# First phase of an attention kernel: x loaded ahead of the values' weights, their scales taken later

## The chip, the cores and the metric

The kernel runs on one core of a Trainium2 chip. The metric is the device time of one execution in microseconds (us), the median of repeated runs. The core's engines are named as the profile names them: PE (TensorE, matrix products), DVE (VectorE), ACT (ScalarE), POOL (GpSimd) and SP (SyncE, which here only issues DMAs).

## The reference, cut to what matters

```
x: (1, 2048, 640), wqkv: (640, 1920), wo: (640, 640), two sets A and B, gate_w: (640)
g = sigmoid((x * gate_w).sum(-1, keepdims=True))
attention(x, wqkv, wo):            # 32 heads of 20 columns
    q, k, v = split of x @ wqkv
    p = softmax(q @ k.T * 20 ** -0.5)
    return (p @ v, heads side by side) @ wo
out = g * attention(x, wqkv_A, wo_A) + (1 - g) * attention(x, wqkv_B, wo_B)
```

Everything is float32, and both attentions read the same x.

## The kernel before

**Numbers.** Matrix products of float32 data are made from float16 pairs. A tensor is multiplied by a power of two that its largest absolute value sets, and split into a high and a low half; a product takes three float16 products (high by high, low by high, high by low). The scale needs a maximum over the whole tensor, so it can't be known before all of the tensor has arrived. The generator `scales` turns a column of per-partition maxima into scales: PE transposes the column (L173), DVE reduces it and forms the power of two and its inverse in six small instructions (L177 to L183), PE spreads both over all partitions (L190), DVE copies them out (L193). It yields `PRODUCT` ahead of each of its two PE steps, so that a caller can place other work between.

**Order.** The program is written out by hand, engine by engine: each engine's instructions run in the order in which the code issues them, and waits follow from the data. There are seven PSUM banks (`take`, `give`): a small model of the engines' clocks chooses which bank is used next; it does not change the order.

**First phase.** SP issues the loads: the first columns of the queries' and keys' weights (`ws`), the values' weights of the first eight heads (`wv`, 160 columns, the 161st is `gate_w`), then x in eight pieces (`xs`). DVE takes maxima as the pieces land (`largest`, L234). One call of `scales` then serves five columns: queries, keys, values, gate and x. From then on PE transposes x (L869, 80 blocks; 24 of them ahead of the scales), ACT writes the scaled high half `xh` (L873) and DVE the low half `xl` (L874).

**Products of the first phase.** `a_chunk(ch)` makes keys and part of the queries of the first four heads for 512 of the 2048 rows: 15 products in one bank, then ACT writes the high half into the staging tile `cq` (L417), DVE the low half (L418), and DMAs spread `cq` into `KT` and `QT` (`kt`, `qt` in the profile), alternately from SP (L428, both halves) and POOL (L430, the high half). Two chunks share one `cq` tile, of which there are two. `r_chunk(ch, ...)` makes the rest of the queries (`rk`) in the same way. `differences_of(half, ...)` forms, on POOL, the differences of two chunks' keys (`fd`, `dd`, L468 to L472) and spreads them into `KD` (`kd`). The order is `a_chunk` 0, 1, 2 (with x's remaining transposes between), `r_chunk(0)`, `a_chunk(3)`, the second differences, and `split_now` for `wv` on ACT and POOL.

**Maxima.** Sixteen groups of four products of queries and keys follow (`max_mm`, L581), each in turn with about six products of the remaining `r_chunk`s and of `project_v`, the values' projection. ACT writes the positive part of one product (L585), DVE adds the other and takes the maximum (L589). The values' projection needs the two halves of `wv`, `wvh` and `wvl`.

**Main loop.** After that a loop of 512 steps makes scores, exponentials and weighted values, with projections and output products filled in. It ends with the output's last rows.

**Constant rows.** Four rows of a constant (`mrow`, in a buffer of the `cq` tag) are copied by four POOL DMAs into rows 60 to 63 and 124 to 127 of both `KT` tiles.

Of the kernel before, what the change touches and what calls it, by code (L numbers as in the profile page):

```python
# [14 lines left out]
OP = mybir.AluOpType  # L15
AX = mybir.AxisListType
# [3 lines left out]
P = 128  # L20
S = 2048
D = 640
# [39 lines left out]
PRODUCT = "product"  # L62
# [6 lines left out]
def kernel(  # L69
# [10 lines left out]
    nc = tc.nc  # L80
# [22 lines left out]
    KT = [consts.tile([P, 2, S], F16, name=f"kt{i}") for i in range(2)]  # L103
# [6 lines left out]
    inv_x = consts.tile([P, 1], F32, name="inv_x")  # L110
    inv_g = consts.tile([P, 1], F32, name="inv_g")
# [17 lines left out]
    def take():  # L129

        i = min((k for k in range(NB) if k not in held), key=lambda k: free_at[k])
        held.add(i)
        return i, banks[i]

    def spend(engine, cost, ready=0.0):

        clock[engine] = max(clock[engine], ready) + cost
        return clock[engine] + T_BACK

    def give(i, t):  # L140
        free_at[i] = t
        held.discard(i)
# [7 lines left out]
    def tick_block(cost, ready=0.0):  # L150

        begin = block_end[0] if now[0] < 0 and block_end[1] == rows_free else max(rows_free) + T_MODE
        clock["pe"] = max(begin, ready)
        rows_free[:] = [clock["pe"] + cost + T_MODE] * 2
        block_end[:] = [clock["pe"] + cost, list(rows_free)]
        clock["done"] = clock["pe"] + cost + T_READY - T_MODE


    def powers(ei, n):

        c = [slice(k * n, (k + 1) * n) for k in range(5)]
        nc.vector.tensor_scalar(ei[:, c[1]], ei[:, c[0]], 0x7F800000, None, op0=OP.bitwise_and)
        nc.vector.tensor_scalar(ei[:, c[2]], ei[:, c[1]], float(20 << 23), None, op0=OP.max)
        nc.vector.tensor_scalar(ei[:, c[3]], ei[:, c[2]], -1.0, float((254 + XE) << 23), op0=OP.mult, op1=OP.add)
        nc.vector.tensor_scalar(ei[:, c[4]], ei[:, c[2]], float(XE << 23), None, op0=OP.subtract)

    def scales(maxima, n, then):

        for _ in range(REST):
            yield  # L170
        yield PRODUCT
        i, pt = take()
        nc.tensor.transpose(pt[:n, :P], maxima[:, :n], ident)  # L173
        tick_block(0.1, free_at[i])
        yield
        e = wts.tile([5, 8], F32, name="e", tag="scl", bufs=2)
        nc.vector.tensor_reduce(e[:n, 0:1], pt[:n, :P], axis=AX.X, op=OP.max)  # L177
        give(i, spend("dve", 0.3, clock["done"]))
        spend("dve", 1.0)
        powers(e.bitcast(I32)[:n, :], 1)  # L180
        dg = wts.tile([5, 2, 5], F32, name="dg", tag="scd", bufs=2)
        for k in range(2):
            nc.vector.tensor_scalar(dg[:n, k, :n], ident[:n, :n], e[:n, 3 + k:4 + k], None, op0=OP.mult)  # L183
        for _ in range(REST):
            yield
        yield PRODUCT
        i, pb = take()
        tick_block(0.1, free_at[i])
        for k in range(2):
            nc.tensor.matmul(pb[:, k * n:(k + 1) * n], ones[:n, :], dg[:n, k, :n], start=True, stop=True)  # L190
        yield
        both = wts.tile([P, 10], F32, name="both", tag="scb", bufs=2)
        nc.vector.tensor_copy(both[:, :2 * n], pb[:, :2 * n])  # L193
        give(i, spend("dve", 0.2, clock["done"]))
        then(both[:, :n], both[:, n:2 * n])
# [12 lines left out]
    def set_v(gg, r, inv):  # L208
        nc.vector.tensor_copy(r_v[gg], r)

        f = gg % (NG // 2) * 160
        while f < (gg % (NG // 2) + 1) * 160:
            p0 = f % P
            n = min(P - p0, (gg % (NG // 2) + 1) * 160 - f, (P, 32, 64, 32)[p0 // 32])
            nc.vector.tensor_copy(wrow[gg // (NG // 2)][p0:p0 + n, f // P:f // P + 1], inv[p0:p0 + n])
            f += n
# [16 lines left out]
    def largest(dst, src):  # L233
        nc.vector.tensor_reduce(dst, src, axis=AX.XY, op=OP.max,  # L234
                                apply_absolute_value=True)
        spend("dve", 0.5)
# [82 lines left out]
    def split_now(t, r, hi, lo):  # L319
        nc.scalar.activation(hi, t, AF.Copy, scale=r)  # L320
        nc.gpsimd.tensor_scalar(t, t, r, None, op0=OP.mult)
        nc.gpsimd.tensor_tensor(lo, t, hi, op=OP.subtract)  # L322
# [97 lines left out]
    def run(gen):  # L420
        for _ in gen:
            pass
# [415 lines left out]
    wv = start.tile([P, NC, 161], F32, name="wv")  # L838
    w_t = wqkv[0].rearrange("(c p) f -> p c f", p=P)
    for part in range(2):  # L840
        nc.sync.dma_start(ws[:, part], w_t[:, :, part * D:part * D + 320])
    nc.sync.dma_start(wv[:, :, :160], w_t[:, :, 2 * D:2 * D + 160])
    for i in range(0, NT, 2):
        nc.sync.dma_start(xs[:, i:i + 2, :], x_t[:, i:i + 2, :])
    nc.scalar.dma_start(wv[:, :, 160], gate_w.rearrange("(c p) -> p c", p=P))
    mrow = wts.tile([P, S], F16, name="mrow", tag="cq", bufs=2)[:4]
    nc.gpsimd.memset(mrow, MS)
    for i in range(2):
        for j in range(2):
            nc.gpsimd.dma_start(KT[i][64 * j + 60:64 * j + 64], mrow.unsqueeze(1).to_broadcast([4, 2, S]))  # L850
    for i in range(2):
        nc.gpsimd.memset(V[i][:, :, :, DH:VW], 1.0)
    xm = start.tile([P, 8], F32, name="xm")
    wm = start.tile([P, 5], F32, name="wm")
    for part in range(2):
        largest(wm[:, part:part + 1], ws[:, part])
    largest(wm[:, 2:3], wv[:, :, :160])
    largest(wm[:, 3:4], wv[:, :, 160:161])
    for i in range(8):
        largest(xm[:, i:i + 1], xs[:, 2 * i:2 * i + 2, :])  # L860
    nc.vector.tensor_reduce(wm[:, 4:5], xm, axis=AX.X, op=OP.max)

    def turn(j0, c):

        n = slice(j0 * P, (j0 + 4) * P)
        i, pt = take()
        for u in range(4):
            tick_block(0.11, free_at[i])
            nc.tensor.transpose(pt[:, u * P:(u + 1) * P], xs[:, j0 + u, c * P:(c + 1) * P], ident)  # L869

        def drain():
            give(i, spend("dve", T_MAX, spend("act", T_EXP, clock["done"])))
            nc.scalar.activation(xh[:, c, n], pt, AF.Copy, scale=r_x)  # L873
            nc.vector.scalar_tensor_tensor(xl[:, c, n], pt, r_x, xh[:, c, n], op0=OP.mult, op1=OP.subtract)  # L874

        return drain

    def turns_of(j0, cs=range(NC)):
        for c in cs:
            turn(j0, c)()  # L880
            yield
# [3 lines left out]
    load()  # L885
    drains = [turn(0, c) for c in range(NC)] + [turn(4, 0)]
    found = []
    run(scales(wm, 5, lambda r, inv: found.extend((r, inv))))
    r, inv = found
    r_x = r[:, 4:5]  # L890
    hi, lo = blk["a", 0] = block_tiles("a")
    split_now(ws[:, 1, :, 0:GF], r[:, 1:2], hi[:, :, 0:GF], lo[:, :, 0:GF])
    split_now(ws[:, 0, :, 0:48], r[:, 0:1], hi[:, :, GF:P], lo[:, :, GF:P])
    for f in drains:
        f()
    hi, lo = blk["r", 0] = block_tiles("r")
# [3 lines left out]
    nc.gpsimd.tensor_copy(hi.rearrange("p c (j f) -> p c j f", j=4), w_r)  # L900
    nc.gpsimd.tensor_tensor(lo.rearrange("p c (j f) -> p c j f", j=4), w_r, hi.rearrange("p c (j f) -> p c j f", j=4),
                            op=OP.subtract)
    nc.vector.tensor_copy(inv_x, inv[:, 4:5])
    halves = []
    both = cycle((nc.sync, nc.gpsimd))

    def a_chunk(ch):
        if ch % 2 == 0:
            halves.append(half_tiles(0))
        n = slice((ch % 2) * QB, (ch % 2 + 1) * QB)  # L910
        hl = halves[ch // 2][:, :, n]
        yield from project_chunk(blk["a", 0], hl[:, 0], hl[:, 1], ch)
        for pair in range(2):
            run(spread(0, hl, ch * QB, QB, q=(0,) if ch == pair == 0 else (), k=(pair,), queues=both))

    def r_chunk(ch, pairs):
        yield from project_r(0, ch)
        n = slice((ch % 2) * QB, (ch % 2 + 1) * QB)
        run(spread(0, halves[ch // 2][:, :, n], ch * QB, QB, q=pairs, k=(), queues=both))
        spread_done.add((0, ch))  # L920

    def beside(gen, n, other):

        for k, _ in enumerate(gen):
            if k % n == n - 1:
                next(other, None)
        run(other)
# [10 lines left out]
    beside(a_chunk(1), 3, turns_of(8))  # L938
    differences_of(0, KD[0])
    beside(a_chunk(2), 3, turns_of(12))  # L940
    run(r_chunk(0, (1,)))
    run(a_chunk(3))
    differences_of(1, KD[1])
    hi, lo = v_tiles(0)
    split_now(wv[:, :, :160], r[:, 2:3], hi[:, :, :160], lo[:, :, :160])
    split_now(wv[:, :, 160:161], r[:, 3:4], hi[:, :, 160:161], lo[:, :, 160:161])
    nc.vector.tensor_scalar(inv_g, inv[:, 3:4], inv_x, -1.0, op0=OP.mult, op1=OP.mult)
    set_qk(0, r[:, 0:2], inv[:, 0:2])
    set_v(0, r[:, 2:3], inv[:, 2:3])
    split_next()  # L950
    rest = series(*(r_chunk(ch, (0, 1)) for ch in (1, 2, 3)), *(project_v(0, j) for j in range(0, NT, 2)))

# [13 lines left out]
    chain = finish_max(0, 0)  # L966
# [25 lines left out]
    for g in range(2 * NG):  # L992
        b = g * step
        n = g + 1
        if n < 2 * NG:
# [5 lines left out]
            i = g // 4 + 1  # L1001
            if i < 4:
                if g % 4 == 0:
                    z, c0 = i // 2, 320 * (i % 2)
                    srcs = max_tasks([[(wqkv[z], part * D + c0 + 160 * k) for k in range(2)] for part in range(2)],
                                     lambda m, i=i: scales_qk(i, m))
# [105 lines left out]
    for G in range(STEPS + 1):  # L1112
        g, qb, i = unit_of(G)
# [12 lines left out]
        for what in (STEP[blocks] if maxima or some else LATE + " X" * (blocks == 2)).split():  # L1126
            k = count[what] = count.get(what, 0) + 1
            if what[0] == "e":
                q = sum(count.get(f"e{j}", 0) for j in range(2)) - 1
                j = int(what[1])  # L1130
# [55 lines left out]
```

## Time and profile before

| | before |
|---|---|
| median of 3 runs | 2802.12 us (2801.08 to 2802.19) |
| the profiled execution's own time | 2800.33 us |
| its span | 2798.5 us, 61863 instructions |
| granted PE clock, mean | 0.995 |
| busy: PE, DVE, ACT, POOL | 98%, 88%, 90%, 24% |

The page gives the busy time of each engine and the chain of work that ended last. Since the change touches only the first phase, the views with a time window are of most use: the timeline (when each instruction began, how long it took, and in brackets how long its engine was idle ahead of it and what ended that), the chain of waits in order of time, and the table of stretches with the granted PE clock and the DMA rate.

### The profile page before, as it was taken

Reading aid. Unit: us, or ns where it says so; the run is one execution under the profiler, and the core shown is the slowest. Engines: PE = TensorE matmul, PEld = TensorE weight load, DVE = VectorE, ACT = ScalarE, POOL = GpSimd, SP = SyncE. Lnnn points to the kernel's source line nnn. Section 1 sums busy time; section 2 is a strip of 40 time slices with the busy share of each in tenths; the row PEclk is TensorE's granted clock in tenths of the full one; section 3 lists DMA queues with packets and bytes.
Section 4 is the critical chain, followed back from the end, with each engine's and each line's share of the span. In section 5 each row is a group of like instructions: output and inputs, shape, how many; then the busy total and the mean of one; then the engine's idle time right before and its main releaser. Section 6 shows DMA issues by size and latency. Waiting matters only on the chain.

```text
span 2798.5 us, 61863 instructions
## 1 busy us (share of the span) xinstructions
PE 2744.9 (98%) x23122; PEld 939.9 (34%) x23122; DVE 2452.3 (88%) x4795; ACT 2524.6 (90%) x5106; POOL 671.9 (24%) x914
## 2 busy tenths in 40 slices
PE   6999999999999999999999999999999999999998
PEld 3433332333333332333333323333333333322222
DVE  6789899889999999888888988989988898999982
ACT  3799999999999999999999889999999999989987
POOL 5322122312222421321221212222342202200111
PEclk9999999999999999999999999999999999999999
DMA  4020102001020211202012231122201112131112
GB/s 136 19 57 14 41 11 46 7 21 25 14 64 17 62 27 54 48 8 61 21 35 70 58 77 31 38 63 54 61 23 42 33 46 63 31 88 55 42 48 75
DMA packets 172943, 124.57 MB, mean 45 GB/s; under 512 B 103264, under 2 KB 142488, under 8 KB 172640
## 3 DMA queue, kind: packets, MB, share of 16 engines
q1 hardware_dynamic: 170096, 118.99, 16.9%
q8 instruction: 181, 2.97, 0.4%
q0 software_dynamic: 1600, 0.96, 0.2%
q14 instruction: 122, 1.00, 0.1%
q10 hardware_dynamic: 944, 0.66, 0.1%
HBM read 54.54 MB, written 31.85 MB: 31 GB/s over the span
## 4 chain that ended last, share of the span: by engine, by line
PE 92%; DVE 3%; ACT 2%; DMA 1%; POOL 1%; issue 1%; SPq 0%; POOLq 0%; ACTq 0%; DVEq 0%
PE acc L657 35%; PE bank L581 19%; PE bank L382 19%; PE bank L639 18%; DVE mpart L592 2%; ACT pt L642 1%; DMA xs<-in_A_x_dram 0%; ACT rl L585 0%; DMA wv<-in_A_wqkv_dram 0%; PE bank L820 0%; DVE rl L589 0%; PE bank L190 0%; SPq L428 0%; DVE ot L743 0%; PE bank L869 0%
## 5 line engine op out<-in xcount | busy, mean ns | idle before, releaser
L642 ACT ACTIVATE pt<-bank 128x512 f32<-128x512 f32 x4096 | 2169.2, 612 | 166.7 <-PE bank L639 101.7
L592 DVE TENSOR_REDUCE mpart<-bank 128x1 f32<-128x512 f32 x2976 | 1865.2, 682 | 222.2 <-PE bank L581 114.8
L657 PE MATMUL acc<-pt,v 128*21 128x512 f32 x8192 | 1082.2, 600 | 0.6 <-DVE ot L743 0.4
L639 PE MATMUL bank<-qt,kt 64*128 64x512 f16 x4096 | 1051.7, 380 | 4.2 <-ACT pt L642 2.0
L581 PE MATMUL bank<-kt,qt 60*128 60x512 f16 x3536 | 1021.3, 380 | 5.1 <-ACT pt L642 1.7
L581 PEld LDWEIGHTS <-qt 60*128 60x128 f16 x4096 | 238.1, 94 | 862.9 <-issue 802.9
L589 DVE CUSTOM_DVE_ANT_0 rl<-bank,rl 128x512 f32<-128x512 f32 x560 | 378.7, 680 | 16.7 <-ACT rl L585 10.6
L585 ACT ACTIVATE rl<-bank 128x512 f32<-128x512 f32 x560 | 329.7, 595 | 10.7 <-PE bank L581 8.7
L639 PEld LDWEIGHTS <-kt 64*128 64x128 f16 x4096 | 235.5, 94 | 238.7 <-issue 122.8
L382 PE MATMUL bank<-xx,wbh 128*128 128x168 f16 (+3 forms) x2400 | 286.0, 239 | 2.6 <-ACT xx L873 1.9
L657 PEld LDWEIGHTS acc<-pt,v 128*21 128x21 f32 x8192 | 143.1, 99 | 428.8 <-issue 421.9
L382 PE MATMUL bank<-xx,wbl 128*128 128x168 f16 (+3 forms) x1200 | 256.1, 237 | 0.0
L751 POOL TENSOR_TENSOR ot<-ot,sq 128x512 f32<-128x512 f32 x63 | 66.0, 1047 | 773.4 <-DVE sq L748 773.4
L382 PEld LDWEIGHTS <-wbh 128*128 128x128 f16 x2400 | 189.4, 98 | 109.5 <-issue 102.0
L581 PE MATMUL bank<-kd,qt 60*128 60x512 f16 x560 | 203.8, 380 | 1.6 <-DMA kd<-dd 1.2
L382 PE MATMUL bank<-woh,o_in 128*128 128x320 f16 (+1 forms) x640 | 156.4, 302 | 5.5 <-DMA o_in<-o_scr 5.4
L411 POOL CAST cq<-fs 128x512 f16<-128x512 f32 x60 | 36.6, 610 | 521.0 <-ACT fs L409 517.4
L382 PE MATMUL bank<-wvh,xx 128*128 128x160 f16 (+1 forms) x1280 | 155.2, 234 | 0.1
L382 PEld LDWEIGHTS <-xx 128*128 128x128 f16 x1920 | 131.5, 97 | 52.3 <-issue 49.1
L382 PE MATMUL bank<-wvl,xx 128*128 128x160 f16 (+1 forms) x640 | 137.3, 231 | 0.5 <-POOL wvl L322 0.5
L382 PEld LDWEIGHTS <-wbl 128*128 128x128 f16 x1200 | 117.4, 98 | 4.3 <-issue 0.8
L382 PEld LDWEIGHTS <-o_in 128*128 128x128 f16 (+1 forms) x960 | 80.9, 97 | 97.7 <-issue 63.8
(131 smaller groups left out, 1259.1 us busy)
## 6 DMA issues: line engine op xcount, KB each, us to landing
y_scr<-y_out SPq DMA_DIRECT2D x48, 320.0 KB
y_out<-y_scr SPq DMA_DIRECT2D x32, 320.0 KB
kt<-cq SPq DMA_DIRECT2D x120, 80.0 KB
o_scr<-on SPq DMA_DIRECT2D x240, 40.0 KB
o_in<-o_scr SPq DMA_DIRECT2D x64, 96.0 KB
kt<-cq SPq DMA_DIRECT2D x136, 40.0 KB
wstage<-in_B_wqkv_dram SPq DMA_DIRECT2D x13, 400.0 KB
xs<-in_A_x_dram SPq DMA_DIRECT2D x8, 640.0 KB
```

Of the source, the lines that this page charges most:

```text
L382: nc.tensor.matmul(out_ap, a, b, start=(k == 0), stop=(k == len(pairs) - 1))
L411: nc.gpsimd.tensor_copy(hi, f)
L581: nc.tensor.matmul(pt, QT[g % 2][r, pair, q0:q0 + P], k, start=True, stop=True)
L585: nc.scalar.activation(relus[u, j], pt, AF.Relu)
L589: nc.vector.tensor_tensor_reduce(rl, pt, rl, 1.0, LOW, OP.add, OP.max, m)
L592: nc.vector.tensor_reduce(m, pt, axis=AX.X, op=OP.max)
L639: nc.tensor.matmul(et, KT[g % 2][r, pair, kt * P:(kt + 1) * P], QT[g % 2][r, pair, qb * QB:(qb + 1) * QB], start=True, stop=True)
L642: nc.scalar.activation(pt, et, AF.Exp, scale=factor(g // 4))
L657: nc.tensor.matmul(acc[32 * h:32 * h + VW, :], V[(g // 2) % 2][:, kt, (g % 2) * GH + h, :], ptiles.pop((G, kk, h)), start=(kt == 0), stop= ...
L751: nc.gpsimd.tensor_tensor(t3, t3, sq.unsqueeze(2).to_broadcast([P, 16, 32]), op=OP.mult)
```

## The change

The load of `wv` is issued behind the eight pieces of x. The load of `gate_w` (on ACT's queue) and the four DMAs of the constant rows (on POOL's) are issued behind the first scaled copies of x and the split of `ws`. The first call of `scales` serves three columns. The maxima of `wv` and of the gate stand behind the last scaled copies of x, and a second call of `scales` serves them: its transpose stands behind the products of `r_chunk(0)`, then a call of `a_chunk(3)`, then its second PE step. The call of `a_chunk(3)` that stood there before stands there still.

```
@@ the loads and the first maxima
-    nc.sync.dma_start(wv[:, :, :160], w_t[:, :, 2 * D:2 * D + 160])
     for i in range(0, NT, 2):
         nc.sync.dma_start(xs[:, i:i + 2, :], x_t[:, i:i + 2, :])
-    nc.scalar.dma_start(wv[:, :, 160], gate_w.rearrange("(c p) -> p c", p=P))
+    nc.sync.dma_start(wv[:, :, :160], w_t[:, :, 2 * D:2 * D + 160])
     mrow = wts.tile([P, S], F16, name="mrow", tag="cq", bufs=2)[:4]
     nc.gpsimd.memset(mrow, MS)
-    for i in range(2):
-        for j in range(2):
-            nc.gpsimd.dma_start(KT[i][64 * j + 60:64 * j + 64], mrow.unsqueeze(1).to_broadcast([4, 2, S]))
...
-    largest(wm[:, 2:3], wv[:, :, :160])
-    largest(wm[:, 3:4], wv[:, :, 160:161])
     for i in range(8):
         largest(xm[:, i:i + 1], xs[:, 2 * i:2 * i + 2, :])
-    nc.vector.tensor_reduce(wm[:, 4:5], xm, axis=AX.X, op=OP.max)
+    nc.vector.tensor_reduce(wm[:, 2:3], xm, axis=AX.X, op=OP.max)
...
-    run(scales(wm, 5, lambda r, inv: found.extend((r, inv))))
+    run(scales(wm, 3, lambda r, inv: found.extend((r, inv))))
...
-    nc.vector.tensor_copy(inv_x, inv[:, 4:5])
+    nc.vector.tensor_copy(inv_x, inv[:, 2:3])
+    nc.scalar.dma_start(wv[:, :, 160], gate_w.rearrange("(c p) -> p c", p=P))
+    for i in range(2):
+        for j in range(2):
+            nc.gpsimd.dma_start(KT[i][64 * j + 60:64 * j + 64], mrow.unsqueeze(1).to_broadcast([4, 2, S]))
...
@@ the chunks
     beside(a_chunk(2), 3, turns_of(12))
+    largest(wm[:, 3:4], wv[:, :, :160])
+    largest(wm[:, 4:5], wv[:, :, 160:161])
     run(r_chunk(0, (1,)))
+    of_v = []
+    chain = scales(wm[:, 3:5], 2, lambda r, inv: of_v.extend((r, inv)))
+    while next(chain) is not PRODUCT:
+        pass
+    next(chain)
+    run(a_chunk(3))
+    while next(chain) is not PRODUCT:
+        pass
+    next(chain)
+    run(chain)
+    rv, invv = of_v
     run(a_chunk(3))
     differences_of(1, KD[1])
     hi, lo = v_tiles(0)
-    split_now(wv[:, :, :160], r[:, 2:3], hi[:, :, :160], lo[:, :, :160])
-    split_now(wv[:, :, 160:161], r[:, 3:4], hi[:, :, 160:161], lo[:, :, 160:161])
+    split_now(wv[:, :, :160], rv[:, 0:1], hi[:, :, :160], lo[:, :, :160])
+    split_now(wv[:, :, 160:161], rv[:, 1:2], hi[:, :, 160:161], lo[:, :, 160:161])
```

SP's queue at the start of the program, as a difference (− before, + now):

```order
 L841 DMA ws<-in_A_wqkv_dram 128x5x320 x2
-L842 DMA wv<-in_A_wqkv_dram 128x5x160
-L844 DMA xs<-in_A_x_dram 128x1280 x8
+L843 DMA xs<-in_A_x_dram 128x1280 x8
+L844 DMA wv<-in_A_wqkv_dram 128x5x160
 L343 DMA wstage<-in_A_wqkv_dram 128x5x80
```

The load of `wv` moved past the eight loads of x.

DVE behind the low half of the keys of chunk 2 (the first `cq` row), before:

```order
L418 SCALAR_TENSOR_TENSOR cq<-bank_95,cq 128x512
L418 SCALAR_TENSOR_TENSOR rk<-bank_93,rk 128x512
L418 SCALAR_TENSOR_TENSOR cq<-bank_94,cq 128x512
L947 TENSOR_SCALAR inv_g<-both,inv_x 128x1
L202 COPY r_qk_99<-both 128x2
```

The same place now:

```order
L418 SCALAR_TENSOR_TENSOR cq<-bank_95,cq 128x512
L234 TENSOR_REDUCE wm<-wv 128x1 x2
L418 SCALAR_TENSOR_TENSOR rk<-bank_93,rk 128x512
L418 SCALAR_TENSOR_TENSOR cq<-bank_89,cq 128x512
L177 TENSOR_REDUCE e<-bank_94 2x1
L162 TENSOR_SCALAR e<-e 2x1
L163 TENSOR_SCALAR e<-e 2x1
L164 TENSOR_SCALAR e<-e 2x1
L165 TENSOR_SCALAR e<-e 2x1
L183 TENSOR_SCALAR dg<-ident,e 2x2 x2
L193 COPY both<-bank_90 128x4
L418 SCALAR_TENSOR_TENSOR cq<-bank_91,cq 128x512
```

The two maxima and the second call of `scales` came in, and a second row writes `cq` for chunk 3 (from bank 91).

ACT from the high half of chunk 2 on, with the semaphores that each row waits for (`DMAHW` of DMAs that SP or ACT issued, `DMASW` of those that POOL issued), before:

```order
L417 ACTIVATE cq<-bank_95 128x512 [waits DMASW2_49,DMASW1_49,DMASW3_49,DMASW0_49,Pool_49]
L417 ACTIVATE rk<-bank_93 128x512 [waits PE_49]
L417 ACTIVATE cq<-bank_94 128x512 [waits PE_49]
L320 ACTIVATE wvh<-wv,both 128x5x160 [waits DMAHW3_49]
L320 ACTIVATE wvh<-wv,both 128x5 [waits DMAHW0_49]
L585 ACTIVATE rl_500<-bank_89 128x512 [waits PE_49]
```

The same place now:

```order
L417 ACTIVATE cq<-bank_95 128x512 [waits DMASW2_49,DMASW1_49,DMASW3_49,DMASW0_49,Pool_49]
L417 ACTIVATE rk<-bank_93 128x512 [waits PE_49]
L417 ACTIVATE cq<-bank_89 128x512 [waits PE_49]
L417 ACTIVATE cq<-bank_91 128x512 [waits DMASW4_49,DMAHW3_49,DMASW3_49,DMAHW4_49,DMASW2_49,DMAHW5_49,DMASW1_49,DMAHW6_49,DVE_49,PE_49]
L320 ACTIVATE wvh<-wv,both 128x5x160 [waits DMAHW2_49,DVE_49]
L320 ACTIVATE wvh<-wv,both 128x5
L585 ACTIVATE rl_539<-bank_92 128x512 [waits PE_49]
```

The second row from bank 91 came in; it overwrites the part of `cq` that the first one wrote, and waits for the eight DMAs that read it. SP and POOL each issue eight `kt` DMAs for chunk 3 instead of four. Behind this place the four engines' instructions and SP's DMAs stand in the order of before; only bank and buffer numbers differ.

More of the change, by code (lines that the diff above doesn't have):

```diff
@@ L887 @@
     found = []
-    run(scales(wm, 5, lambda r, inv: found.extend((r, inv))))
+    run(scales(wm, 3, lambda r, inv: found.extend((r, inv))))
     r, inv = found
-    r_x = r[:, 4:5]
+    r_x = r[:, 2:3]
     hi, lo = blk["a", 0] = block_tiles("a")
@@ L944 @@
     hi, lo = v_tiles(0)
-    split_now(wv[:, :, :160], r[:, 2:3], hi[:, :, :160], lo[:, :, :160])
-    split_now(wv[:, :, 160:161], r[:, 3:4], hi[:, :, 160:161], lo[:, :, 160:161])
-    nc.vector.tensor_scalar(inv_g, inv[:, 3:4], inv_x, -1.0, op0=OP.mult, op1=OP.mult)
+    split_now(wv[:, :, :160], rv[:, 0:1], hi[:, :, :160], lo[:, :, :160])
+    split_now(wv[:, :, 160:161], rv[:, 1:2], hi[:, :, 160:161], lo[:, :, 160:161])
+    nc.vector.tensor_scalar(inv_g, invv[:, 1:2], inv_x, -1.0, op0=OP.mult, op1=OP.mult)
     set_qk(0, r[:, 0:2], inv[:, 0:2])
-    set_v(0, r[:, 2:3], inv[:, 2:3])
+    set_v(0, rv[:, 0:1], invv[:, 0:1])
     split_next()
```

## The prediction

> **What bounds the kernel now.** I read the page first, for what a stretch of lost time is worth.
>
> ```profile
> PE 2744.9 (98%) x23122; PEld 939.9 (34%) x23122; DVE 2452.3 (88%) x4795; ACT 2524.6 (90%) x5106; POOL 671.9 (24%) x914
> ```
>
> PE is busy 98% of the span, and behind the first phase every engine's order is unchanged. So what the first phase gains or loses should reach the end one for one; there is no slack in 2.7 ms of main loop to swallow it. Then the chain that ended last, in its first 100 us (start, duration, what):
>
> ```profile
> 1.79 11.17 DMA wv<-in_A_wqkv_dram
> 12.97 12.94 DMA xs<-in_A_x_dram
> ...
> 55.23 2.25 DMA kd<-dd
> 57.62 0.71 PE bank L581 x4
> ...
> 95.97 3.05 DMA wstage<-in_A_wqkv_dram
> ```
>
> The first 26 us are loads: `wv`, then x. At 57.6 the groups of maxima start, behind a `kd` DMA.
>
> **The lead of x.** The timeline of DVE, and two PE steps of `scales`:
>
> ```profile
> 9.50 1.82 DVE L234 TENSOR_REDUCE wm<-ws 128x1 f32<-128x1600 f32 x1 [1.43 <-DMA ws<-in_A_wqkv_dram]
> 12.98 1.05 DVE L234 TENSOR_REDUCE wm<-wv 128x1 f32<-128x800 f32 x2 [1.65 <-DMA wv<-in_A_wqkv_dram]
> 14.73 10.98 DVE L234 TENSOR_REDUCE xm<-xs 128x1 f32<-128x1280 f32 x7 [0.70 <-DMA xs<-in_A_x_dram]
> 25.93 1.49 DVE L234 TENSOR_REDUCE xm<-xs 128x1 f32<-128x1280 f32 x1 [0.23 <-DMA xs<-in_A_x_dram]
> 27.67 0.38 PE L173 MATMUL bank<-ident,wm 128*5 128x128 f32 x1 [6.38 <-DVE wm L861]
> 28.08 0.28 DVE L177 TENSOR_REDUCE e<-bank 5x1 f32<-5x128 f32 x1 [0.47 <-PE bank L173]
> 29.27 1.01 PE L190 MATMUL bank<-dg,ones 5*128 5x5 f32 x4 [1.23 <-DVE dg L183]
> ```
>
> The last of `ws` lands at 9.50, `wv` at 12.98 (3.48 later, though it is only 400 KB), the first x at 14.73. Without `wv` ahead, x lands 3.48 sooner, at 11.25; DVE is free at 9.50 + 1.82 = 11.32. So x starts at 11.32, 3.41 earlier, and from there the eight pieces keep their pace, since DVE and DMA are nearly level on them (7 in 10.98 us). The 1.05 us of `wv` maxima go with it. What else leaves the front:
>
> ```profile
> 5.00:5.50 0.50, 0.00 (x0) 0.00 (x0) 0.00 (x0) 0.00 (x0) 0.50 (x2) 1.00 0.54 104
> 5.50:6.00 0.50, 0.00 (x0) 0.00 (x0) 0.00 (x0) 0.00 (x0) 0.50 (x2) 1.00 0.76 221
> 12.50:13.00 0.50, 0.00 (x0) 0.00 (x0) 0.02 (x1) 0.00 (x0) 0.00 (x0) 1.00 1.08 418
> ...
> q10 hardware_dynamic: 363, 0.00, 13.5%
> ...
> q10 hardware_dynamic: 261, 0.00, 9.3%
> ```
>
> (Stretches with DMA share and GB/s last; then the queue of `gate_w` in 3.5 to 5.0 and 5.0 to 6.5.) The gate's packets took 1.5 × (13.5% + 9.3%) = 0.34 us of the DMA engines, and beside them these were idle for 0.5 × 0.46 + 0.5 × 0.24 = 0.35. So the gain is 3.4 to 4.1; I take 3.9. The low end is the bytes alone, 410 KB at 418 GB/s = 1.0; the landings themselves are the nearer row. DVE, PE and ACT stages up to the chunks all move by this. The gate's DMA issue on ACT and the constant rows' issue on POOL are costed at nothing: the first lies in a place where ACT waits for PE, the second (2.51 us, below) is covered by POOL's idle 2.77 ahead of 46.06. Three columns instead of five in `scales` change no duration.
>
> **Chunk 3 is made twice.** From here I use the times of before, and take off the 3.9 at the end.
>
> ```profile
> 53.06 2.32 PE L382 MATMUL bank<-xx,wbh 128*128 128x512 f16 x10
> 55.22 1.24 PE L382 MATMUL bank<-xx,wbl 128*128 128x512 f16 x5
> 56.49 0.60 ACT L417 ACTIVATE cq<-bank 128x512 f16<-128x512 f32 x1 [2.64 <-PE bank L382]
> 56.99 1.16 ACT L320 ACTIVATE wvh<-wv,both 128x800 f16<-128x800 f32 x2
> 58.03 1.08 ACT L585 ACTIVATE rl<-bank 128x512 f32<-128x512 f32 x2
> ...
> 53.62 3.19 SPq L428 DMA_DIRECT2D kd<-dd  x4
> 56.91 3.19 SPq L428 DMA_DIRECT2D kt<-cq  x4
> 62.69 3.20 SPq L428 DMA_DIRECT2D kt<-cq  x4
> ...
> 59.01 2.00 POOL L430 DMA_DIRECT2D kt<-cq  x4
> 61.02 1.17 POOL L468 TENSOR_TENSOR fd<-cq 80x512 f32<-80x512 f16 x1
> 73.00 0.22 POOL L322 TENSOR_TENSOR wvl<-wv,wvh 128x5 f16<-128x5 f32 x1
> ...
> 59.67 0.39 PE L581 MATMUL bank<-kd,qt 60*128 60x512 f16 x2
> 61.60 0.39 PE L581 MATMUL bank<-kd,qt 60*128 60x512 f16 x2
> 72.50 0.23 PE L382 MATMUL bank<-wvh,xx 128*128 128x161 f16 x1
> 73.28 0.23 PE L382 MATMUL bank<-wvl,xx 128*128 128x161 f16 x1 [0.55 <-POOL wvl L322]
> ```
>
> The 15 extra products cost PE 3.4 us (53.06 to 56.46). But PE is not what ends last. The second `cq` row on ACT waits until the first pass's `kt` DMAs have read `cq`. SP issues one every 0.80 us, and chunk 3's four stand behind `kd`, chunk 2 and three `qt` DMAs: SP starts them at 62.69, whenever the chunk was ready. The last is issued at 62.69 + 3 × 0.80 = 65.1 and lands 2.25 later (the `kd` piece of the chain at 55.23): 67.3. So:
>
> - ACT writes `cq` the second time at 67.4 instead of 56.49, 10.9 later. Queued behind it are both `wvh` and every ACT row of the maxima: the first runs at 58.03 + 10.9 = 68.9.
> - POOL's second four `kt` start at 67.4 + 0.6, end at 70.0; `fd` starts there instead of at 61.02, 9.0 later, and `wvl`, ready at 73.22, is ready at 82.2.
> - PE has by then made one group of maxima and stands, since a bank is given back only by ACT. Its second group goes on at 68.9 + 0.6 = 69.5 and takes 1.93 (59.67 to 61.60), so the third starts at 71.5 instead of 61.60: 9.9 late. At the values' first product PE is at 72.50 + 9.9 = 82.4, where `wvl` is ready and the wait of 0.55 is gone: the product of 73.28 runs at 82.5, 9.2 late.
>
> The second `scales` chain (L173 to L193) hides whole under this stall: PE would be through chunk 3's second pass by 64.2 (below).
>
> **The clock.** Stretches late in the first phase (PE busy and granted clock):
>
> ```profile
> 97.00:98.00 1.00, 0.58 (x5) 1.00 0.74 129
> ...
> 100.00:101.00 1.00, 0.92 (x5) 0.70 0.00 0
> 101.00:102.00 1.00, 1.00 (x5) 0.50 0.00 0
> ```
>
> After about 3 us in which PE was partly idle, its clock fell to half. My stall leaves PE idle from about 66 to 69.5, so the next groups should run at half clock for one 3.4 us stretch; half speed on 3.4 us costs up to 1.7, some of it under ACT's start: I take 1.5 (0 to 2.6). [...]
>
> **Sum.** 9.2 + 1.5 − 3.9 = **+6.8 us**. On the profiled execution 2800.33 + 6.8 = 2807.1; that execution lies 1.8 below the median, so the forecast on the median is 2802.12 + 6.8 = **2808.9**, 0.24% slower. A difference of 0.2%, 5.6 us, is about what a measurement of this kernel can tell from none.
>
> **Rivals.**
>
> - *The clock holds.* PE's one group and its products inside the stall count as busy. 9.2 − 3.9 = +5.3: 2807.4, just inside 0.2%.
> - *The constant rows land late.* Rows:
>
> ```profile
> 37.89 1.41 POOL L901 TENSOR_TENSOR wbl<-ws,wbh 128x640 f16<-128x640 f32 x1
> 46.06 1.99 POOL L430 DMA_DIRECT2D kt<-cq  x4 [2.77 <-ACT cq L417]
> 3.46 2.51 POOL L850 DMA_DIRECT2D kt<-mrow  x4 [0.31 <-POOL mrow L847]
> ...
> kt<-mrow POOLq DMA_DIRECT2D x4, 32.0 KB, 7.1
> ```
>
>   They now issue from 39.3 to 41.8, and later `kt` issues on POOL wait for their landing. If that takes 7.1 us as before, the fourth lands at 39.3 + 1.9 + 7.1 = 48.3, the last two of the four `kt` at 46.06 start then, and POOL comes out 1.7 late; so do `kd` and SP's queue. +8.5: 2810.6. Against it: the 7.1 were taken while `ws` and x filled the DMA engines.
> - *SP's backlog does not gate* (the other side: not slower). If the first pass's `kt` DMAs land before PE's second pass ends, PE sets the time: 53.06 + 3.4 + 0.4 (transpose) is 56.9, ACT 0.6, DVE about 0.7, 1.2 from L177 to the second PE step (28.08 to 29.27), that step 1.0, again 3.4, with hand-overs 64.2. The maxima start at 64.2 instead of 57.62, POOL's `fd` at 66.9; the product of 73.28 runs at 79.2, 5.9 late, and the sum is +2.0: 2804.1. It decides if the DMAs land 3.1 us sooner than I reckon, at 64.2; SP's unbroken row of issues from 53.62 speaks against.
> - *The shift is swallowed later.* In the chain the `wstage` load at 95.97 holds DVE for up to 3.05 us; were its start not tied to the maxima, then with the case before the sum is −1: 2801. SP's order puts it behind the maxima's own DMAs, so I give this little.
>
> **How the numbers follow.** Forecast 0.53, clock holds 0.15, late rows 0.12, no gating 0.13, swallowed or a larger lead of x 0.07. Slower by over 0.2%: most of the forecast (0.45), some of the clock case (0.06) and nearly all of the late rows: 0.62. Faster: the last case and a little of the others: 0.08. Within 0.2%: 0.30. The range goes from 2802.5 (no gating, with 1.6 for its parts) to 2814 (late rows with the clock's 2.6 and 2 us less gain on x).
>
> **What would show it.** Right: x's first maximum at about 11 us, ACT's second chunk-3 `cq` row with an idle of several us ended by a `kt` DMA, PE idle about 3 us behind the first group of maxima, half clock after it. Wrong: that ACT row released by PE; x's first maximum later than 13; or a distance between the two traces at the maxima that is gone by 150 us.

## The result and the profile after

| | before | after |
|---|---|---|
| median of 15 runs | 2801.97 us (2800.3 to 2804.24) | 2807.47 us (2805.82 to 2808.84) |
| ratio, 95% interval | | 1.0020 (1.0012 to 1.0027) |
| the profiled execution's own time, span | 2800.33, 2798.5 | 2807.05, 2805.3 |

The changed kernel is 5.5 us slower on the medians and 6.7 on the two profiled executions. The chain that ended last, in its first 100 us:

```profile
1.24 6.50 DMA ws<-in_A_wqkv_dram
7.75 12.69 DMA xs<-in_A_x_dram
...
60.88 0.76 SPq L428
61.68 2.12 DMA kt<-cq
64.40 1.16 ACT wvh L320 x2
```

Before, the last of `wv` and x had landed at 25.9; now the last of `ws` and x has at 20.4. And where the `kd` DMA led to the maxima, SP's `kt` issues now lead to ACT. The timeline of DVE:

```profile
7.76 1.82 DVE L234 TENSOR_REDUCE wm<-ws 128x1 f32<-128x1600 f32 x1 [0.42 <-DMA ws<-in_A_wqkv_dram]
9.49 12.45 DVE L234 TENSOR_REDUCE xm<-xs 128x1 f32<-128x1280 f32 x8
21.98 0.16 DVE L855 TENSOR_REDUCE wm<-xm 128x1 f32<-128x8 f32 x1
```

The second part of `ws` landed 1.74 us sooner. The eight maxima of x run almost without a gap, and the last of them still starts when x's last piece has landed (20.44 in the chain): DVE and the loads are level there. The reduction over them starts at 21.98 instead of 27.45, a lead of 5.47 us. Not all of it reaches the chunks. ACT's first `cq` row, before and then now:

```profile
39.18 0.60 ACT L417 ACTIVATE cq<-bank 128x512 f16<-128x512 f32 x1 [0.82 <-PE bank L382]
...
34.54 0.60 ACT L417 ACTIVATE cq<-bank 128x512 f16<-128x512 f32 x1 [0.82 <-PE bank L382]
```

And the granted clock of PE (third figure), again before and then now:

```profile
35.00:36.00 1.00, 1.00 (x7) 0.72 0.00 0
...
31.00:32.00 1.00, 1.00 (x7) 0.60 0.00 0
```

Here the lead is 4.64. DVE has the scales ready 5.48 us sooner (24.84 instead of 30.32), but PE, whose granted clock is 0.50 from 25.3 us before and from 18.1 now, gets its whole clock back only 3.75 us sooner (31.8 instead of 35.55). Half speed for 1.73 us more is worth 0.86 by my estimate, about what the lead lost. Then POOL, SP, ACT and PE:

```profile
38.70 0.51 POOL L430 DMA_DIRECT2D kt<-cq  x1 [0.34 <-DMA kt<-mrow]
40.81 0.51 POOL L430 DMA_DIRECT2D kt<-cq  x1 [1.60 <-DMA kt<-mrow]
42.59 2.00 POOL L430 DMA_DIRECT2D kt<-cq  x4 [1.28 <-DMA kt<-mrow]
...
50.17 3.19 SPq L428 DMA_DIRECT2D kd<-dd  x4
59.24 9.35 SPq L428 DMA_DIRECT2D kt<-cq  x8
...
52.02 0.60 ACT L417 ACTIVATE cq<-bank 128x512 f16<-128x512 f32 x1 [2.80 <-PE bank L382]
63.91 0.60 ACT L417 ACTIVATE cq<-bank 128x512 f16<-128x512 f32 x1 [11.29 <-DMA kt<-cq]
...
66.08 0.58 PE L581 MATMUL bank<-kd,qt 60*128 60x512 f16 x1 [3.84 <-ACT rl L585]
80.54 0.23 PE L382 MATMUL bank<-wvl,xx 128*128 128x161 f16 x1
```

POOL stood three times for the landing of the constant rows, 3.22 us in all. The `kd` DMAs leave 3.45 us sooner than before (53.62 to 50.17): of the lead of 4.64 at ACT's first row, POOL took another 1.2. SP starts chunk 3's `kt` at 59.24, and ACT's second `cq` row stands 11.29 us, until 63.91, for their landing. PE then stands 3.84 us. The first product with `wvl` runs at 80.54 instead of 73.28, 7.26 late; the span ends 6.8 late. The granted clock behind PE's wait:

```profile
65.00:66.00 1.00, 0.00 (x0) 0.97 0.10 29
66.00:67.00 1.00, 0.92 (x3) 0.50 0.28 61
...
69.00:70.00 1.00, 1.00 (x6) 0.83 0.18 41
```

It is half (0.50) from 66.0 to 69.3. Behind the maxima the distance between the two traces shrinks once. Two rows of ACT that follow one another, before and then now:

```profile
96.77 0.32 ACT L409 ACTIVATE fs<-bank 128x176 f32<-128x176 f32 x1 [0.81 <-PE bank L382]
104.36 0.31 ACT L409 ACTIVATE fs<-bank 128x168 f32<-128x168 f32 x1 [1.01 <-PE bank L382]
...
104.04 0.32 ACT L409 ACTIVATE fs<-bank 128x176 f32<-128x176 f32 x1 [0.81 <-PE bank L382]
110.52 0.31 ACT L409 ACTIVATE fs<-bank 128x168 f32<-128x168 f32 x1
```

The first is 7.27 late, the second 6.16. Between them the execution of before ran at a granted clock of 0.50 (100.4 to 103.8); the changed one did the same work at 1.00 (104 to 110). So 1.1 of the 7.27 us went for a reason that has nothing to do with the second pass, and the 6.2 that are left are nearly the whole of the 6.8 at the end.

### The profile page after: what moved, and what is told of

The parts are those of the page before. It is cut to its first block, busy times and chain, and to the rows that moved or that the text cites. A ratio compares the mean times of both kernels' runs of the same rounds, so it can differ in the third digit from the quotient of the medians.

```text
span 2805.3 us, 61941 instructions
## 1 busy us (share of the span) xinstructions
PE 2751.8 (98%) x23142; PEld 941.9 (34%) x23142; DVE 2452.6 (87%) x4804; ACT 2524.5 (90%) x5107; POOL 673.7 (24%) x918
## 4 chain that ended last, share of the span: by engine, by line
PE 92%; DVE 3%; ACT 2%; SPq 1%; DMA 1%; issue 1%; POOL 0%; POOLq 0%; ACTq 0%; DVEq 0%
PE acc L657 34%; PE bank L382 20%; PE bank L581 19%; PE bank L639 18%; DVE mpart L592 2%; ACT pt L642 1%; SPq L428 1%; DMA xs<-in_A_x_dram 0%; SPq L430 0%; ACT rl L585 0%; PE bank L820 0%; DVE rl L589 0%; PE bank L190 0%; PE bank L863 0%; DMA ws<-in_A_wqkv_dram 0%
```

## The experiments

**The second pass alone.** The kernel before, with chunk 3 made twice:

```
     run(a_chunk(3))
+    run(a_chunk(3))
```

> The kernel before with a second call of a_chunk(3) right behind the first, and nothing else. Theory of the forecast: ACT's second cq row stands until the first pass's kt DMAs have landed at about 67.3 us (SP's queue has the same backlog as before); the products with wvl run 9.2 us late, with the half clock after the stall 10.7: about 2812.5, between +9 and +12. Rival (the second pass costs what its products cost PE): 3.4 us less the 1.16 us for which PE waited for kd anyway: +2.3.

Measured: 2813.63 us against 2801.64, ratio 1.0045 (1.0028 to 1.0061). The timeline of ACT and PE:

```profile
67.56 0.60 ACT L417 ACTIVATE cq<-bank 128x512 f16<-128x512 f32 x1 [10.27 <-DMA kt<-cq]
...
69.73 0.58 PE L581 MATMUL bank<-kd,qt 60*128 60x512 f16 x1 [7.58 <-ACT rl L585]
```

The ACT row starts at 67.56, against 67.3 expected. The pass costs about 12 us, at the upper end of the 9 to 12 expected and not the 2.3 of its products: the rival falls.

**The same passes without the wait.** In the changed kernel, the first pass writes a tile of its own:

```
-    run(a_chunk(3))
+    own = start.tile([P, 2, QB], F16, name="cq0")
+    first = project_chunk(blk["a", 0], own[:, 0], own[:, 1], 3)
+    run(first)
+    for pair in range(2):
+        run(spread(0, own, 3 * QB, QB, q=(), k=(pair,), queues=both))
```

> The changed kernel, but the first pass of chunk 3 writes a tile of its own, from which its kt DMAs read; the second pass writes cq and has no earlier readers to wait for. The same work on every engine and as many DMAs. Theory of the forecast (the wait for the readers gates): ACT's second row follows PE's second pass at about 58.5 to 60 us instead of 63.9, POOL's differences start at 62.6, and the product of 73.28 before runs at about 74.9: +1.6 against before (0 to +3), 4 to 6 us below the changed kernel. Rival (PE's products, its clock or SP's extra DMAs set the time): as the changed kernel, +5.5.

Measured: 2804.24 us against 2801.64, ratio 1.0009 (1.0 to 1.0019); 3.2 us below the changed kernel's median. ACT's row now follows PE:

```profile
60.41 0.60 ACT L417 ACTIVATE cq<-bank 128x512 f16<-128x512 f32 x1 [7.41 <-PE bank L382]
...
75.74 0.23 PE L382 MATMUL bank<-wvl,xx 128*128 128x161 f16 x1
```

All products and DMAs are still there; the first product with `wvl` runs at 75.74 instead of 80.54. Of these 4.8 us, 3.5 are the wait of the second `cq` row for the readers of the first (60.41 against 63.91); the rest fits the half clock behind that wait (66.0 to 69.3 in the changed kernel), which this kernel doesn't have there (1.00 from 60 to 78). Against the kernel before it came out 1 us above the expected 1.6, but within its range. Against the changed kernel 3.2 us are short of the 4 to 6 expected: of the 4.8 us, 2.9 are left at the end of the two profiled spans (2802.4 against 2805.3), and what took the rest is not shown.

**Once instead of twice.** The changed kernel without its second call:

```
     rv, invv = of_v
-    run(a_chunk(3))
```

> The changed kernel without the second call of a_chunk(3); the loads, the second scales chain and its two PE steps stay. Theory of the forecast (the second pass and its wait for the first pass's kt DMAs are the price): the maxima start when the chain's second PE step is through, at about 55.0 us instead of 57.62 before, wvl is ready 3.5 us sooner than before, and the first product with it runs at 70.0 instead of 73.28. So about 3.3 us faster than before, 10 us below the changed kernel. Rival (the price is the second scales chain, for which PE stood 2.38 us and spent 0.60): only the 3.4 us of the second pass's products come back, and the kernel stays about 2 to 3 us slower than before.

Measured: 2802.16 us against 2801.64, ratio 1.0002 (0.9993 to 1.0012): no gain over the kernel before. My 3.3 us did not come. Timeline and clock of PE:

```profile
53.36 0.79 PE L190 MATMUL bank<-dg,ones 2*128 2x2 f32 x4 [2.38 <-DVE dg L183]
54.08 0.61 PE L581 MATMUL bank<-kd,qt 60*128 60x512 f16 x2
...
74.99 0.24 PE L382 MATMUL bank<-wvh,xx 128*128 128x161 f16 x1
...
53.00:54.00 1.00, 0.64 (x4) 0.81 0.40 97
54.00:55.00 1.00, 1.00 (x5) 0.50 0.30 70
...
63.00:64.00 1.00, 1.00 (x3) 0.57 0.33 74
```

The maxima start at 54.08 instead of 57.62, 3.5 us sooner, but after PE's wait of 2.38 us for the second `scales` chain the clock is half (0.50) from about 53.5 to 63.9, and `project_v` starts at 74.99 instead of 72.50. Of the 6.0 us that go between the two places, half speed on 10.2 us can account for 5.1; PE also stands 0.95 and 0.26 us for ACT's rows of the maxima. The rival had the right place, the second chain, with the wrong price: not the wait but what follows it.

**PE kept busy in that wait.** The same kernel with twelve unused products:

```
     run(a_chunk(3))
+    i, pt = take()
+    for k in range(12):
+        nc.tensor.matmul(pt, blk["a", 0][0][:, 0, :], xh[:, 0, 0:QB], start=True, stop=True)
+    give(i, free_at[i])
     while next(chain) is not PRODUCT:
```

> The kernel with chunk 3 made once, and 12 spare products of 512 columns (2.6 us, their results unused) on PE between chunk 3 and the second PE step of the scales chain, where PE stood 2.38 us. Theory (the half clock took the gain of the kernel with chunk 3 made once: after that wait it ran its first groups of maxima at half clock from 53.5 to 64): with PE busy there the clock stays whole, the maxima start at 54.3 as before and the first product with wvl runs at about 69.7 instead of 75.0; 5 us below that kernel, 3 to 4 us below the kernel before (2798). Rival (something else holds these groups, ACT's or DVE's rows behind the late scales): no gain, 2802, and the spare products cost 0.2 us.

Measured: 2801.03 us against 2801.99, ratio 0.9998 (0.9989 to 1.0007). The expected 3 to 4 us did not come, and the rival's 2802 lies as near:

```profile
54.00 0.39 PE L581 MATMUL bank<-kd,qt 60*128 60x512 f16 x2
55.99 0.81 PE L382 MATMUL bank<-xx,wbh 128*128 128x512 f16 x3 [1.38 <-ACT rl L585]
...
54.30 1.17 ACT L320 ACTIVATE wvh<-wv,both 128x800 f16<-128x800 f32 x2 [2.72 <-DVE both L193]
...
56.00:57.00 1.00, 1.00 (x6) 0.99 0.36 87
57.00:58.00 1.00, 0.74 (x4) 0.50 0.24 52
...
63.00:64.00 1.00, 1.00 (x4) 0.59 0.32 74
```

The clock held 3.4 us longer (it fell at 53.6 in the kernel without the spare products) and was half from 57.0 to 63.9, behind a second wait of 1.38 us: `wvh` waits 2.72 us for the late scales as well, and stands on ACT ahead of the maxima's rows. So theory and rival each held a part: the first groups ran at half clock again, and PE's wait ahead of it was for ACT's rows behind the late scales.

**The chain ahead of chunk 3's rows.** Chunk 3 once, and DVE's part of the chain issued ahead of chunk 3's `cq` row, which mends both waits:

```
     next(chain)
-    run(a_chunk(3))
     while next(chain) is not PRODUCT:
         pass
+    run(a_chunk(3))
     next(chain)
```

> Chunk 3 made once, and DVE's part of the second scales chain issued ahead of chunk 3's cq row, so that PE's second step stands ready when chunk 3's products end. Theory: PE's wait of 2.38 us is gone, the maxima start when kd lands at about 52.8, after a wait of about 1 us as in the kernel before, so the clock holds; wvl is ready at 68.5, 4.7 us sooner than before, and that sets the first product with it. 4.7 us below the kernel before: 2797.3 (2795.5 to 2799). Rival (the clock falls in PE's wait for kd anyway): 2800 to 2802.

Measured: 2797.51 us against 2801.99, ratio 0.9985 (0.9976 to 0.9994).

```profile
52.45 0.60 PE L190 MATMUL bank<-dg,ones 2*128 2x2 f32 x4
53.63 0.50 PE L581 MATMUL bank<-kd,qt 60*128 60x512 f16 x2 [0.58 <-DMA kd<-dd]
69.25 0.23 PE L382 MATMUL bank<-wvl,xx 128*128 128x161 f16 x1 [0.28 <-POOL wvl L322]
...
53.00:54.00 1.00, 0.42 (x5) 1.00 0.36 85
```

From 47 to 77 us PE's longest wait is 0.58, the granted clock is 1.00 from 50 to 66, and the first product with `wvl` runs 4.0 us sooner than before (4.7 expected); the time came within 0.3 us of the expected 2797.3. This is the change without the second pass and with the chain in time, and it beats both kernels. Since it takes away PE's wait and ACT's late rows together, their shares are not told apart.

**The constant rows back at the front.** The changed kernel with the four DMAs at their old place (the loop moved back behind `memset(mrow, MS)`):

> The changed kernel with the four DMAs of the constant rows back at their old place, ahead of everything on POOL. In the changed kernel POOL stood 0.34, 1.60 and 1.28 us for their landing, and its differences came 3.45 us sooner than before though x came 5.5 sooner. Theory (the rows' late landing takes 2.0 us of the lead of x): POOL's waits vanish, the kd and kt DMAs and with them ACT's second cq row come 2.0 us sooner against x; x itself comes later by what the rows' packets cost at the front, 0 to 1.7 us. So 0.3 to 2.0 us below the changed kernel, x's first maximum between 9.5 and 11.2. Rival (POOL's waits are covered): the kernel is the changed one's or up to 1.7 us slower, with ACT's second cq row as late after x's last maximum as now.

Measured: 2811.14 us against 2801.64, ratio 1.0033 (1.002 to 1.0045), 3.7 above the changed kernel. DVE, and the DMA rate from 8 to 9.5 us:

```profile
12.15 1.49 DVE L234 TENSOR_REDUCE xm<-xs 128x1 f32<-128x1280 f32 x1 [2.38 <-DMA xs<-in_A_x_dram]
25.23 0.16 DVE L858 TENSOR_REDUCE wm<-xm 128x1 f32<-128x8 f32 x1
...
8.00:9.50 1.50, 0.00 (x0) 0.00 (x0) 1.50 (x1) 1.27 (x1) 0.00 (x0) 1.00 1.03 221
```

The same stretch of the changed kernel:

```profile
8.00:9.50 1.50, 0.05 (x1) 0.08 (x2) 1.50 (x2) 1.09 (x1) 0.00 (x0) 1.00 1.02 416
```

The first half of the theory held: POOL's waits vanish, and ACT's second `cq` row comes 40.1 us behind x's reduction instead of 41.9, so 1.8 us sooner against x, where 2.0 was expected. The second half missed, and the rival's bound with it: x's reduction starts 3.25 us later than in the changed kernel (25.23 against 21.98), almost twice my bound of 1.7. While the rows are under way, all DMAs together move 221 GB/s, against 416 in that stretch of the changed kernel, though the DMA engines are as busy (1.03 and 1.02).

**The gate's load back at the front**, one execution:

> The changed kernel with only the load of gate_w back at its old place, first on ACT's queue. One look at the first 25 us. In the changed kernel the second part of ws landed 1.74 us sooner than before, where the forecast had given gate and rows together at most 0.7. If the gate's packets are the cause, ws lands at 9.2 to 9.5 again and x's last maximum ends 1.5 to 1.7 us later than in the changed kernel; if the rows' packets are, ws lands at 7.7 to 8 and x's last maximum ends as in the changed kernel (with the rows early and the gate late, ws landed at 7.94 and x's last maximum ended 3.25 later).

```profile
9.01 1.82 DVE L234 TENSOR_REDUCE wm<-ws 128x1 f32<-128x1600 f32 x1 [1.13 <-DMA ws<-in_A_wqkv_dram]
...
23.24 0.16 DVE L856 TENSOR_REDUCE wm<-xm 128x1 f32<-128x8 f32 x1
```

`ws` landed at 9.01 instead of 7.76, and x's reduction started at 23.24, 1.26 us after the changed kernel's. So the gate's load makes up 1.25 of the 1.74 us, a little less than expected. The time of this execution, 2811.21 us, is above all those of the changed kernel (2805.82 to 2808.84), but one execution doesn't price the load.

**Only `wv` moved**, in the kernel before, one execution:

> The kernel before with only the load of wv behind x, and its maxima behind x's; gate and constant rows stay first, and one scales call serves all five columns. One look at the loads. In the changed kernel x's last maximum ended 5.47 us sooner than before; with the gate back early 1.26 of that was gone, with the rows back early 3.25. If these add up, wv alone leads x by about 1.0 us (its bytes at the rate of x), and x's last maximum ends near 26.4 instead of 27.42. The forecast's own reading, that the 3.4 us between the landings of ws and wv are all wv's, gives 24.0.

```profile
25.57 0.16 DVE L859 TENSOR_REDUCE wm<-xm 128x1 f32<-128x8 f32 x1
```

x's reduction started 1.88 us sooner than before: between the 1.0 of the sum and the 3.4 of the forecast. The three leads are 1.88 (`wv` alone moved), 1.26 and 3.25 (gate and rows, each alone moved back); together 6.4 against 5.47, so they overlap, and each alone is no share of the whole. What can be said is that moving gate and rows as well brought another 3.59 (25.57 to 21.98), the larger part. Of the 1.88, only 0.43 was left in the maxima (the third group starts at 61.17 instead of 61.60), since the maxima of `wv`, 1.05 us, now stand between x's and the scales. The time was 2800.31 us, against 2802.05 for the kernel before beside it: within what executions of the kernel before differ by (2800.18 to 2804.34).

**The rows behind the split of `wv`.** The kernel with the chain ahead, the rows in a tile of their own (`mrow` from `start`), their DMAs ahead of the second `split_next()`:

> As the kernel with the chain ahead, with the constant rows in a tile of their own and their four DMAs behind the split of wv on POOL. Theory: POOL no longer stands 0.27 and 1.68 us for the rows' landing, nor spends 2.5 us on them ahead of chunk 0's kt DMAs; kd lands 2 us sooner, before PE needs it, so the maxima start when chunk 3 and PE's step are through, at about 51.7, and wvl is ready 2 us sooner. 5.5 to 6.5 us below the kernel before, 1 to 2 below the kernel with the chain ahead. Rival: the rows' issue and landing now delay POOL's qt DMAs, on which later groups wait: no gain over that kernel.

Measured: 2796.49 us against 2801.99, ratio 0.9981 (0.9972 to 0.999): the lowest median here. Against the kernel with the chain ahead it is 1.0 lower, less than the two intervals tell apart. The theory's 2 us did not come: `kd`'s DMAs leave 0.8 us sooner (48.74 against 49.52 on POOL), since POOL now stands 2.73 us for ACT's `cq` row instead; PE still waits 0.49 us for `kd`, and the maxima start at 52.82, not 51.7.

## Why the prediction was right, and where its sizes were off

The range held the result, and the time moved as forecast: 2807.47, against 2808.9. The mechanism that was named, the wait of ACT's second row, is the one that the runs show. That the sum came so near is in part luck: x led by 1.6 us more than I took, and 2.0 us of its lead were lost again on the way to `kd`. Point by point:

- *The second pass gates through the `kt` DMAs, not through its products.* Shown by the three kernels in which the second pass is alone, has no readers to wait for, and is gone. ACT's second row was reckoned at 67.4 in the times of before; with the pass alone it stood at 67.56. In the changed kernel it came at 63.9 (63.5 with the forecast's lead taken off).
- *The clock falls behind the stall.* Right: a granted clock of 0.50 from 66.0 to 69.3, about as long as in the kernel before (100.4 to 103.8). That a stall brings one such stretch and no more was my estimate; in the kernel with chunk 3 made once the clock was half for about 10 us (53.5 to 63.9). The price of 1.5 fits: the third group of maxima starts at 69.58, where the forecast, with the measured lead of 3.45, has 68.05 at whole clock. No run takes this fall away by itself; the one of before at 100.4 cost 1.1. An earlier fall in the second pass (0.50 from 55.7 to 59.1) lay under ACT's wait, and I had not named it. The stretch ahead of the fall on which the forecast rested, 97.0 to 100.4 in the kernel before, was far from idle: PE was busy for 2.58 of its 3.41 us.
- *The lead of x is 3.9.* Wrong in size: 5.47. I had bounded gate and rows by the time of their packets, 0.34 us for the gate, and given all 3.4 us between the landings of `ws` and `wv` to `wv`; `wv` alone moved leads by 1.88, and beside the rows' DMAs all DMAs together moved 221 GB/s instead of 416.
- *The constant rows' issue is covered by POOL's idle 2.77.* Wrong. The rival of late rows came true in its place: they land in 6.3 us with little beside them (63 GB/s in all from 35 to 42 us), so most of the 7.1 of before was not a matter of load, and POOL stood 3.22 us. Of the lead of 5.47, 0.8 was gone at ACT's first `cq` row, which the half clock behind the scales can account for (0.86), and POOL took 1.2; `kd` kept 3.45. The errors met: the sum took 3.9 off, the chain 3.45.
- *The sum.* 9.2 + 1.5 − 3.45 = 7.25, against 7.26 at the first product with `wvl`. At the end 6.8 are left, after the 1.1 us that went at 104 us. On the medians it is 5.5, since the profiled execution of before lay 1.6 below its median, the one after only 0.4.
- *The other rivals.* No gating and a whole clock did not happen. Of the shift, 1.1 us was swallowed later, where the clock of before was half and the changed one's whole, and not at the `wstage` load.

## What to carry to other kernels

A tile that is written again is free when its readers are through, and if the readers are DMAs that stand in a backlogged queue, that can be late: ACT stood 11.29 us ahead of such a row here, 3.5 of them for the readers alone. Look up where they stand in the queue, not when their data was ready. When a wait on PE is shortened or moved, look at the granted clock behind it: the kernel with chunk 3 made once started its maxima 3.5 us sooner and ended no sooner, with the clock at 0.50 from about 53.5 to 63.9. A fall of the clock that comes in one execution and not in the next (1.1 us here) can also pass for a part of a small effect. And small DMAs that run beside a large load should be priced by the load's rate while they run (221 GB/s in all instead of 416 beside the constant rows), not by their own bytes.

## What was not expected of the hardware

- PE's clock fell after stretches in which PE was far from idle. In the kernel with the spare products it fell to 0.50 behind 3.4 us (53.6 to 57.0) with PE busy for 2.02, and stayed there through the next 3.4 with PE busy for 3.15. The busy time of such a stretch alone doesn't tell: in the kernel before, 2.25 of 3.41 us (56.03 to 59.44, with the wait of 1.16) left the clock whole (1.00) and 2.58 (97.00 to 100.41) did not, and the changed kernel did the work of the latter (104.27 to 107.68, again 2.58) without a fall. In the changed kernel's trace the clock changes at 55.7, 59.1, 65.9 and 69.3, so 3.4 us or a multiple apart. The stretches compared have the length of the half clock of before (100.41 to 103.82); where they begin was my choice, and what decides on a fall is not shown.
- Four DMAs of 32 KB each, to four partitions each, took 6.3 us to land (the median) in the changed kernel, where all DMAs together moved 63 GB/s (35 to 42 us). Beside the loads they took 7.1 (before) and 8.4 (back at the front), and in the latter kernel all DMAs together moved 221 GB/s while they ran (8.0 to 9.5 us) against 416 in that stretch of the changed kernel. The changed kernel's row:

```profile
kt<-mrow POOLq DMA_DIRECT2D x4, 32.0 KB, 6.3
```

- The load of `gate_w`, 2.5 KB, delayed x by 1.26 us (in one execution), though its packets took 0.34 us of the DMA engines' time (read in the kernel before).
